# ScalarE's list of small jobs in the down product: the two relus of the big pass's lower right quarter moved ahead by two and one places, with an empty job between them

## The chip, the cores and the metric

One core of one Trainium2 chip. The time is device microseconds of one execution; the kernel before took a median of 957.89 us in 3 runs (957.74 to 960.14). The profile is of one further execution, whose span is 954.6 us.

## The reference, cut to what matters

```python
# x: (8, 4224, 192)
w = softmax(weight)                       # (8 heads, 7 taps)
x = sum over k of w[h, k] * x_padded[:, s + k, head h]     # causal convolution along s
mu, var = mean and variance of x over its 192 columns
xn = (x - mu) / sqrt(var + 1e-6) * g_ln
out = x + relu(xn @ w_ch1) @ w_ch2        # w_ch1: 192 x 768, w_ch2: 768 x 192
```

All in float32.

## The kernel before

The 8 x 4224 rows are cut into 18 groups: three small ones to start with and, from group 3 on, groups of 128 x 16 rows. For each group VectorE makes the convolution (L417, with ScalarE making the first two taps, L380 and L398), the rows are transposed in 32 x 32 blocks, TensorE makes the first product ("up", L533), the relu follows, TensorE makes the second product ("down", L850), and the result is scaled by 1/sqrt(var) (L929) and added to the output, where the convolution already stands, by a DMA that accumulates (L940).

For the groups from 3 on both products are made by a 2 x 2 block scheme in which seven products of quarters stand in for eight. In the up product (`up_mixed`) this is done in two passes: the small pass `one`, over one of three chunks of the hidden units, and after it the big pass `two`, over the other two. Each pass leaves four quarters of the hidden matrix in the tile `room`: c11, c12 (upper) and c21, c22 (lower). The quarter c22 of the big pass is put together from a copy out of PSUM (L651) and a second copy, which goes to a side tile called `parts_tb`, and which GpSimd's queue then adds into `room` by one accumulating DMA of 1024 KB (L609). A relu in place must follow that DMA. It is made by ScalarE (L664) in two halves of 128 x 1024, one for each of the big pass's two hidden chunks.

The down product (`down_fast`) is seven products, each of three output chunks (c = 0, 1, 2). A chunk of a product is 3 hidden chunks x 4 row blocks = 12 matmuls, which the profile records as 24, so that a product has 72 records. Inside an output chunk the hidden chunk of the small pass comes first, then the two of the big pass. The first product reads the upper left quarter, the second the lower left one, and the third the lower right one, c22, with all its relus made. After each output chunk ScalarE copies the PSUM bank away (L856), except after the fourth product. The second and third products use the same three banks: the third accumulates on what the second left, and so may write a bank only after ScalarE has copied it.

What else ScalarE has to do stands in a list of small jobs, `work`, from which `product` takes a written-out number of jobs right after the copy of each output chunk: `behind` = 3 jobs a chunk in the first product, 2 in the second, 2 in the third, 3 in the fourth, then 2 in the fifth and sixth until the list is empty. `up_mixed` makes the list's first part for groups 3 to 16 (14 groups; the last group, 17, has a list of its own): the relu of the small pass's c22, then the scalings of rows 2 to 15 of the group before (`scale_one`; after row 7 and the last row the rows go out by DMA), and the two halves of the big pass's c22 put in at a fixed place. `down_fast` appends 16 jobs for the first two taps of the group after next, 8 `first_tap` and 8 `second_tap`, where there is such a group. Engines run their instructions in the order in which the program issues them.

With the list before, the first product's nine places hold the small relu and scalings 2 to 9; the two halves are the two jobs after the copy of the second product's first chunk; scalings 10 to 15 and the taps follow.

Of the kernel before, what the change touches and what calls it, by code (L numbers as in the profile page):

```python
# [16 lines left out]
def kernel(  # L17
# [593 lines left out]
    def up_mixed(g, ahead, pending):  # L611
# [167 lines left out]
        work = [lambda: one.relu(one.c22)]  # L779
        work += [lambda j=j: scale_one(j) for j in range(2, done)]  # L780
        half = [lambda i=i: two.relu(two.c22[:, i : i + 1]) for i in range(PAIR)]
        return work[0:9] + half + work[9:]

    def down_row(rows, left):

# [210 lines left out]
    def ahead(g):  # L996


        if results is not None:
            for half in range(2):  # L1000
                finish_fast(g - 1, half, *results)
        yield
# [3 lines left out]
    for g in range(NG):  # L1006
# [3 lines left out]
        if mixed:  # L1010
            work = up_mixed(g, ahead(g), pending)
            pending = iter(())
        else:
            up(g)
            work = []
# [90 lines left out]
```

## Time and profile before

| what | value |
|---|---|
| time, median of 3 runs | 957.89 us (957.74 to 960.14) |
| span of the profiled execution | 954.6 us |
| TensorE busy (matmuls) | 946.8 us, 99% |
| VectorE busy | 894.2 us, 94% |
| ScalarE busy | 694.8 us, 73% |
| GpSimd busy | 341.8 us, 36% |
| relus L664, 128 x 1024 | 88 of 1063 ns |
| scalings L929, 128 x 192 | 224 of 464 ns |
| copies L856 to `cs`, 128 x 256 | 168 of 375 ns |
| taps L380 / L398, 128 x 384 | 120 of 634 ns / 112 of 638 ns |
| ScalarE's longest waits: L651 for TensorE (L533) | 98.6 us in 143 waits |

Busy time is the time in which an engine has an instruction running. The page's fourth part follows the work that ended last back to its releasers; its fifth lists groups of instructions with the mean time of one. A timeline gives, for one engine, the start and length of each group of like instructions in order, with the idle time just before it and what ended that. One instruction may start before the one ahead of it on its engine has ended, so a pair of 1.06 us can take 2.01 us.

### The profile page before, as it was taken

Reading aid. Unit: us, or ns where it says so; the run is one execution under the profiler, and the core shown is the slowest. Engines: PE = TensorE matmul, PEld = TensorE weight load, DVE = VectorE, ACT = ScalarE, POOL = GpSimd, SP = SyncE. Lnnn points to the kernel's source line nnn. Section 1 sums busy time; section 2 is a strip of 40 time slices with the busy share of each in tenths; the row PEclk is TensorE's granted clock in tenths of the full one; section 3 lists DMA queues with packets and bytes.
Section 4 is the critical chain, followed back from the end, with each engine's and each line's share of the span. In section 5 each row is a group of like instructions: output and inputs, shape, how many; then the busy total and the mean of one; then the engine's idle time right before and its main releaser. Section 6 shows DMA issues by size and latency. Waiting matters only on the chain.

```text
span 954.6 us, 37896 instructions
## 1 busy us (share of the span) xinstructions
PE 946.8 (99%) x16858; PEld 734.5 (77%) x16858; DVE 894.2 (94%) x1496; ACT 694.8 (73%) x1166; POOL 341.8 (36%) x474
## 2 busy tenths in 40 slices
PE   8999999999999999999999999999999999999998
PEld 7998896877869687786958778695867769586787
DVE  8999999999999999999999999999999999999867
ACT  7764678596877959687796968779695877967362
POOL 1158422613145141533227141452316232261330
PEclk9999999999999999999999999999999999999999
DMA  8359589689696988979697897969889697778261
GB/s 206 111 151 218 110 233 269 122 188 226 130 273 131 251 158 185 221 130 278 126 252 152 199 215 128 277 133 249 158 198 206 124 275 134 174 135 141 40 122 68
DMA packets 39832, 169.34 MB, mean 177 GB/s; under 512 B 4469, under 2 KB 8182, under 8 KB 33655
## 3 DMA queue, kind: packets, MB, share of 16 engines
q0 software_dynamic: 32864, 106.77, 60.2%
q1 hardware_dynamic: 6800, 60.16, 17.4%
q8 instruction: 132, 2.16, 0.9%
q14 instruction: 30, 0.25, 0.1%
q10 hardware_dynamic: 6, 0.00, 0.0%
HBM read 38.93 MB, written 50.33 MB: 94 GB/s over the span
## 4 chain that ended last, share of the span: by engine, by line
PE 96%; DMA 1%; POOL 1%; ACT 1%; issue 0%; DVE 0%; ACTq 0%; POOLq 0%
PE ps L533 46%; PE ps L850 44%; PE ps L787 4%; PE ps L367 1%; DMA room<-room 1%; DMA out_dram<-y 1%; PE ps L326 1%; ACT room L651 0%; POOL room L609 0%; POOL d L460 0%; ACT y L380 0%; POOL r L483 0%; POOL d L478 0%; POOL d L479 0%; PE ps L335 0%
## 5 line engine op out<-in xcount | busy, mean ns | idle before, releaser
L417 DVE SCALAR_TENSOR_TENSOR y<-xg,taps,y 128x384 f32<-128x384 f32 (+3 forms) x720 | 364.8, 583 | 2.6 <-DMA y<-room 1.4
L850 PE MATMUL ps<-room,w2sums 128*32 128x256 f32 (+2 forms) x4608 | 246.6, 371 | 0.0
L533 PE MATMUL ps<-yt,w 32*128 32x256 f32 (+2 forms) x4104 | 234.7, 378 | 1.0 <-ACT room L523 0.5
L533 PEld LDWEIGHTS ps<-yt,w 32*128 32x128 f32 x4104 | 204.2, 185 | 26.3 <-issue 8.7
L651 ACT COPY room<-ps 128x1024 f32<-128x1024 f32 (+1 forms) x129 | 169.0, 1310 | 74.5 <-PE ps L533 73.5
L850 PEld LDWEIGHTS ps<-room,w2sums 128*32 128x32 f32 x4608 | 149.3, 110 | 91.5 <-ACT room L664 5.3
L850 PE MATMUL ps<-room,w 128*32 128x256 f32 (+2 forms) x3456 | 188.9, 371 | 0.0
L817 DVE TENSOR_TENSOR room<-room 128x1024 f32<-128x1024 f32 (+2 forms) x147 | 161.2, 1170 | 22.6 <-PE ps L850 16.0
L850 PEld LDWEIGHTS ps<-room,w 128*32 128x32 f32 x3456 | 110.7, 110 | 70.3 <-DVE room L657 5.0
L533 PE MATMUL ps<-ysums,w1sums 32*128 32x256 f32 x2160 | 124.9, 379 | 0.2 <-issue 0.2
L533 PEld LDWEIGHTS ps<-ysums,w1sums 32*128 32x128 f32 x2160 | 109.5, 185 | 10.5 <-ACT room L651 3.3
L940 POOL DMA_DIRECT2D out_dram<-ot x69 | 59.0, 942 | 155.6 <-ACT ot L929 102.5
L409 POOL DMA_DIRECT2D y<-tb x59 | 52.5, 1386 | 153.5 <-ACT room L856 110.1
L856 ACT COPY cs<-ps 128x256 f32<-128x256 f32 (+2 forms) x192 | 70.1, 367 | 45.2 <-PE ps L850 45.2
L664 ACT ACTIVATE room<-room 128x1024 f32<-128x1024 f32 (+1 forms) x89 | 92.5, 1072 | 1.7 <-DMA room<-parts_cs 0.9
L929 ACT ACTIVATE ot<-ot,r 128x192 f32<-128x192 f32 x224 | 90.9, 464 | 0.0
L380 ACT ACTIVATE y<-xg,taps 128x384 f32<-128x384 f32 (+3 forms) x141 | 73.0, 607 | 1.0 <-DMA out_dram<-y 0.7
L448 DVE BATCH_NORM_STATS2 st<-y 128x6 f32<-128x192 f32 x264 | 70.1, 344 | 0.0
L856 ACT COPY room<-ps 128x256 f32<-128x256 f32 (+2 forms) x96 | 35.5, 370 | 45.8 <-PE ps L850 43.8
L398 ACT ACTIVATE tb<-xg,taps 128x384 f32<-128x384 f32 (+1 forms) x120 | 66.1, 628 | 0.0
L533 PE MATMUL ps<-yt,w1sums 32*128 32x256 f32 x1080 | 65.2, 380 | 0.6 <-ACT room L651 0.6
L533 PE MATMUL ps<-ysums,w 32*128 32x256 f32 x1080 | 64.5, 376 | 0.0
(119 smaller groups left out, 924.8 us busy)
## 6 DMA issues: line engine op xcount, KB each, us to landing
xg<-in_x_dram SPq DMA_DIRECT2D x14, 2112.0 KB, 16.4
room<-room POOLq DMA_DIRECT2D x45, 512.0 KB, 5.1
out_dram<-ot POOLq DMA_DIRECT2D x59, 384.0 KB, 9.6
y<-tb POOLq DMA_DIRECT2D x58, 384.0 KB, 8.4
out_dram<-y SPq DMA_DIRECT2D x13, 1536.0 KB, 8.8
room<-parts_cs POOLq DMA_DIRECT2D x28, 512.0 KB, 6.7
room<-parts_tb POOLq DMA_DIRECT2D x14, 1024.0 KB, 7.6
xg<-in_x_dram POOLq DMA_DIRECT2D x1, 2112.0 KB, 13.8
```

The lines of the kernel that those rows point to most:

```text
L380: nc.scalar.mul(y[g][:, 0:n, cs], xg[g][:, 0:n, cs], taps[:, h, 0:1])
L398: nc.scalar.mul(tb[g][:, 0:n, cs], xg[g][:, 1 : 1 + n, cs], taps[:, h, 1:2])
L417: nc.vector.scalar_tensor_tensor(out=y[g][:, 0:n, cs], in0=t[:, k : k + n, cs], scalar=taps[:, h, k : k + 1], in1=y[g][:, 0:n, cs], op0=AL ...
L448: nc.vector.bn_stats(out=sums[g][:, j, :], in_=y[g][:, j, :])
L533: nc.tensor.matmul(banks[:, q, i * w : i * w + w], right[rows, c, P * i : P * i + P], left[rows, :, c, :], start=(first and c == 0 and i = ...
L651: nc.scalar.activation(dst, src, AF.Relu) if relu else nc.scalar.copy(dst, src)
L664: nc.scalar.activation(c, c, AF.Relu)
L817: nc.vector.tensor_tensor(a[:, *dst, f], a[:, *left, f], a[:, *right, f], op=op)
L850: nc.tensor.matmul(dst[C * q : C * q + C, 0:w], right[:, f, C * c : C * c + C], left[:, f, q], start=(first and f == PAIR), stop=(f == PAI ...
L856: nc.scalar.copy(to[:, c], dst[:, 0:w].rearrange("p (j t) -> p j t", t=t))
L929: nc.scalar.mul(ots[g][:, j, :], ots[g][:, j, :], rstd[g][:, j : j + 1])
L940: nc.gpsimd.dma_start(out=rows[:, d0:d1], in_=src[:, d0:d1], accum_op=ALU.add)
```

## The change

Only the order in which `up_mixed` hands out its list is changed: 7 jobs instead of 9 stand before the first half, an empty job follows it, then the second half, then the rest.

```diff
         work = [lambda: one.relu(one.c22)]
         work += [lambda j=j: scale_one(j) for j in range(2, done)]
         half = [lambda i=i: two.relu(two.c22[:, i : i + 1]) for i in range(PAIR)]
-        return work[0:9] + half + work[9:]
+        return work[0:7] + [half[0], lambda: None, half[1]] + work[7:]
```

With `behind` = (3, 2, 2, 3) the first product's nine places now hold the small relu, scalings 2 to 7, the first half and the empty job; the second product's first chunk is followed by its copy, the second half and scaling 8; its second chunk by scalings 9 and 10; and so on. The list is longer by the empty job, so that each place further on holds the job that stood one place ahead of it.

## The prediction

> **What bounds the kernel now.** I read the page first: span, busy times, the chain that ended last.
>
> ```profile
> span 954.6 us, 37896 instructions
> PE 946.8 (99%) x16858; PEld 734.5 (77%) x16858; DVE 894.2 (94%) x1496; ACT 694.8 (73%) x1166; POOL 341.8 (36%) x474
> PEclk9999999999999999999999999999999999999999
> PE 96%; DMA 1%; POOL 1%; ACT 1%; issue 0%; DVE 0%; ACTq 0%; POOLq 0%
> ```
>
> TensorE sets the end: 96% of the chain is its matmuls, at a granted clock of 0.9 or more throughout. A change on ScalarE can only be worth the time in which TensorE stands or is held back. So I read the list of waits next, for weight loads (PEld) that wait for the moved relus (L664).
>
> ```profile
> PEld ps L850 <- ACT room L664: 5.3, 14, 0.4
> ```
>
> There are 14 such waits, one in each of the groups 3 to 16, 5.3 us together, 0.38 us each. The weight loader runs ahead of the matmuls, so its idle time isn't TensorE's loss. For that I took the timeline of TensorE in one down product, that of the pass from 533.55 us, and of its weight loads (columns: start, length, engine, line, work, count, idle before).
>
> ```profile
> 533.55 4.09 PE L850 MATMUL ps<-room,w 128*32 128x256 f32 x72
> 537.46 8.06 PE L850 MATMUL ps<-room,w2sums 128*32 128x256 f32 x144
> 545.34 4.07 PE L850 MATMUL ps<-room,w 128*32 128x256 f32 x72
> 549.22 7.95 PE L850 MATMUL ps<-room,w2sums 128*32 128x256 f32 x144
> 556.99 4.07 PE L850 MATMUL ps<-room,w 128*32 128x256 f32 x72
> ...
> 537.24 4.66 PEld L850 LDWEIGHTS ps<-room,w2sums 128*32 128x32 f32 x88
> 542.29 2.75 PEld L850 LDWEIGHTS ps<-room,w2sums 128*32 128x32 f32 x56 [0.38 <-ACT room L664]
> ```
>
> Take differences of starts. Products five and six (144 records) take 556.99 - 549.22 = 7.77 us, product four 549.22 - 545.34 = 3.88. Products two and three, the same count as five and six, take 545.34 - 537.46 = 7.88. So the wait costs TensorE 7.88 - 7.77 = 0.11 us a pass. It stands where 88 loads are made: 72 of product two and 16 of product three, that is 8 for the small pass's hidden chunk and 8 for the first half. What is late is the second half's relu, before the load at 542.29. ScalarE in the same pass:
>
> ```profile
> 538.67 0.36 ACT L856 COPY cs<-ps 128x256 f32<-128x256 f32 x1
> 538.93 1.15 ACT L929 ACTIVATE ot<-ot,r 128x192 f32<-128x192 f32 x3
> 539.98 0.36 ACT L856 COPY cs<-ps 128x256 f32<-128x256 f32 x1
> 540.23 2.01 ACT L664 ACTIVATE room<-room 128x1024 f32<-128x1024 f32 x2
> 542.14 0.36 ACT L856 COPY cs<-ps 128x256 f32<-128x256 f32 x1
> ...
> 530.67 0.86 POOL L609 DMA_DIRECT2D room<-parts_tb  x1 [6.86 <-ACT parts_tb L651]
> ...
> DMA to landing us min/median/max: 7.0/7.6/8.8
> ```
>
> The pair of halves ends at 540.23 + 2.01 = 542.24 us and the load starts at 542.29. Above it stand scalings 7, 8, 9 (three in 1.15 us). None of these lines has an idle time in front: ScalarE is behind its work here, not waiting. The last lines are the issue of the DMA that must land before the first half, and the landing times of the 14 such DMAs from their issue.
>
> **The change part by part.** Nothing is computed less or more: the same relus, scalings, copies and taps, in another order.
>
> *What is taken from in front of the second half.* Steps of ScalarE from start to start, by the same lines: a copy 0.25 us (539.98 to 540.23), a scaling 0.35 ((1.15 - 0.46)/2, a scaling being 464 ns), a half relu 0.95 (2.01 - 1.06). New order after the copy at 538.67: scaling 7 at 538.93, first half at 539.28, copy of product two's first chunk at 540.23, second half at 540.48, which ends at 541.54. Then scaling 8 at 541.43, the copy of the second chunk at 541.78, scalings 9 and 10, and the copy of the third at 542.73.
>
> *What TensorE needs.* Product three would start at 537.46 + 3.88 = 541.34. Its 17th matmul comes 16/72 of 3.88 later, at 542.20, and its load 0.22 ahead of that (537.24 against 537.46 at the start of product two), at 541.98. The second half ends at 541.54: 0.44 us early, so that wait is gone. Three others come near it. The first load of product three, at 541.12, needs the first half and the copy of the first chunk's bank, over by 540.23 + 0.36 = 540.59: 0.53 early. The second chunk's bank is needed 8 records of 0.054 us after 541.98, at 542.41; its copy ends at 542.14: 0.27 early. The third's is needed at 543.70 and is copied by 543.09. So the whole 0.11 us goes and nothing takes its place: 14 x 0.11 = 1.5 us.
>
> *The DMA in front of the first half.* This wait is not new, but it now comes sooner: 539.28 - 530.67 = 8.61 us after the issue instead of 9.56. Behind it on ScalarE queue up the three copies for whose banks TensorE waits. The landing took 7.6 us (median), so there is 1.0 us to spare. At the longest, 8.8, the half would wait 0.2 us, which the 0.27 of the tightest copy covers. Cost taken: nothing. If that cover were gone it is one for one: landings of 8.9 us and more hold TensorE.
>
> The Trainium skill ("DMA: Bandwidth & Descriptors", Rules for kernel authors) speaks against this part: issue a DMA early, do compute, wait on its semaphore late. The same page's fit, 2.0 us plus bytes over 436e3 per us, would make 1 MiB land in an estimated 4.4 us, and the sum by it is the same 1.5 us gained. The traced 7.6 decides, and with it the rule still has 1.0 us in hand.
>
> *What is delayed.* Scalings 8 and 9 and all behind them stand further down the list. The copies come 0.25 to 0.5 us sooner, since each place holds one job less before it; the scaling of row 11 and of row 15, after which GpSimd sends rows out, come some 0.25 us later. GpSimd waited in these places for ScalarE anyway (the DMA issues at 543.49 and 545.41), nothing else is queued on it before the taps' DMAs, and VectorE writes the next results (L914) late enough, in the pass from 422.75 us at 452.65 against the last issue at 434.61, 18 us for a landing of 9.6: cost nothing. The taps: as many jobs stand ahead of the first one as before (17) and ahead of the last one too (32), so they are made at the same time; where a copy of products three and five moves, it moves ahead of one tap, to be 0.5 us earlier. SP's queue is not touched.
>
> *What follows a freed TensorE.* VectorE's sums (L817) start when product three ends. VectorE idles 1.02 us there, having ended its transpose at 544.19 for a start at 545.21, so it starts 0.11 sooner and the later products, which wait for these sums, move along. The rest of the pass depends on TensorE alone, and the 1.5 us reach the end.
>
> The sum: 954.6 - 1.5 = 953.1 us of span. Around the span the runs have 957.89 - 954.6 = 3.3 us; so the median goes to 957.89 - 1.5 = 956.4. That is 0.16%, less than the 0.3% (2.9 us) that a measurement of this kernel can tell from no change.
>
> **The bounds.** Both unknowns come from this trace. The gain a pass is 0 if the next copy takes the wait's place, and 0.11 if none does. One pass in this execution had a late DMA on ScalarE (0.99 us before L651 at 748.74, and a TensorE period of 56.3 us against 55.4); whether it happens again changes the time by 0.9 either way. Range: 957.89 - 1.5 - 0.9 = 955.5 below, and no gain with half of that late DMA above, 957.89 + 0.45 = 958.3.
>
> **The rivals.**
>
> *The wait only changes its name: 957.9.* The copy of product two's second chunk has 0.27 us to spare by steps taken from other pairs of neighbours; a relu between two copies isn't in the trace as such. If a copy after a relu came 0.3 us later than reckoned, the load for the second chunk would wait instead. For it: ScalarE is behind throughout this stretch. Against it: in the old order the same copy ended at 542.50 and even that wasn't shown as a wait after the one at 542.29.
>
> *The whole idle time of the loader is gained: 957.9 - 5.3 = 952.6.* For it: the row of waits has 5.3 us, and a loader that is ahead might keep TensorE denser. Against it: TensorE's own starts lose only 0.11, not 0.38, and its matmuls are back to back at 3.88 a product elsewhere. The Trainium skill ("TensorE: Matmul & The Clock Gate", The mechanism) says that weight loads are pulled ahead of running matmuls in a window of 64; by that alone the 0.38 would be wholly hidden and the gain 0, while the trace shows a lead of 0.22 and a loss of 0.11.
>
> *Slower: the first half waits for its DMA, 966.6.* One mechanism, at the first half: from a landing of 8.88 us after issue (8.61 + 0.27) each further microsecond is one on TensorE, 14 times. If the DMA landed as the other accumulating ones of this queue do (`out_dram<-ot`, 9.6 us), it would be 14 x (9.6 - 8.88) = 10.1 us lost against 1.5 gained: 957.9 + 8.6. It decides the sign against 0.3% from a mean landing of 8.88 + (2.9 + 1.5)/14 = 9.2. For it: the queue carries much at that time. Against it: 14 landings between 7.0 and 8.8, and no DMA of the output is issued before the half that wasn't before.
>
> **How the numbers follow.** Forecast (1.5 us gained, 956.4) 0.74; the wait changes its name 0.13; both are within 0.3%, 0.87 together. The larger gain 0.07, which is all of faster. The late DMA 0.06, all of slower. The time is that of the forecast; the range 955.5 to 958.3 takes in the first two cases and leaves the others out.
>
> **What would show it.** In the changed kernel's profile the waits of weight loads at L850 for L664 should be gone from the list, with none for L856 in their place; products two and three should take 7.77 us by their starts; ScalarE should show copy, scaling, relu, copy, relu, scaling, copy without idle time; the period from pass to pass should be 55.29 us instead of 55.40. I am wrong if ScalarE idles before L664 for `parts_tb`, if a weight load waits for L856, or if the products shorten by 0.11 and the end doesn't move, which would mean that another engine holds the pass.

## The result, and the profile after

The changed kernel took 955.51 us (median of 11 runs, 954.57 to 956.52), the kernel before, beside it and earlier, 957.5 us (median of 11, 955.96 to 960.14). The ratio is 0.998, with a 95% interval of 0.9972 to 0.9988: 2.0 us less, by the interval 1.1 to 2.7. Two further comparisons of the same two kernels gave 0.9984 (0.9975 to 0.9992) and 0.9981 (0.9972 to 0.9991). The predicted gain was 1.5 us, 0.9984 of the median before; the forecast was 956.4 us and the range 955.5 to 958.3, so that the median lies just inside its lower end. The interval stays below 1, so 11 runs of each kernel do tell 0.2% from no change, for which the prediction had thought 0.3% necessary.

The page of the changed kernel: span, busy times, the chain that ended last.

```profile
span 953.1 us, 37882 instructions
PE 946.6 (99%) x16858; PEld 742.9 (78%) x16858; DVE 894.4 (94%) x1496; ACT 694.9 (73%) x1166; POOL 341.0 (36%) x474
PE 99%; DVE 0%; DMA 0%; issue 0%; ACT 0%
```

TensorE's matmuls are 99% of the chain, and ScalarE is as busy as it was. From the list of waits of the changed kernel, all the rows of weight loads of the down product (columns: who waited for whom, us in total, times, longest):

```profile
PEld ps L850 <- DVE room L657: 5.0, 15, 0.3
PEld ps L850 <- ACT y L380: 0.4, 1, 0.4
PEld ps L850 <- issue: 0.3, 1, 0.3
PEld ps L850 <- ACT room L651: 0.3, 1, 0.3
```

The row with L664 (5.3 us in 14 waits) is gone, and no row with L856 has come. TensorE and its weight loads in one pass, the timelines of the changed kernel from 533.74 us:

```profile
533.74 4.09 PE L850 MATMUL ps<-room,w 128*32 128x256 f32 x72
537.64 7.95 PE L850 MATMUL ps<-room,w2sums 128*32 128x256 f32 x144
545.41 4.07 PE L850 MATMUL ps<-room,w 128*32 128x256 f32 x72
549.30 7.95 PE L850 MATMUL ps<-room,w2sums 128*32 128x256 f32 x144
557.07 4.07 PE L850 MATMUL ps<-room,w 128*32 128x256 f32 x72
...
537.43 7.68 PEld L850 LDWEIGHTS ps<-room,w2sums 128*32 128x32 f32 x144
```

Products two and three take 545.41 - 537.64 = 7.77 us by their starts, as five and six do; before it was 7.88. The 144 weight loads are one group without an idle time in it. ScalarE in the same pass of the changed kernel:

```profile
538.85 0.38 ACT L856 COPY cs<-ps 128x256 f32<-128x256 f32 x1
539.10 0.47 ACT L929 ACTIVATE ot<-ot,r 128x192 f32<-128x192 f32 x1
539.46 1.06 ACT L664 ACTIVATE room<-room 128x1024 f32<-128x1024 f32 x1
540.41 0.38 ACT L856 COPY cs<-ps 128x256 f32<-128x256 f32 x1
540.66 1.08 ACT L664 ACTIVATE room<-room 128x1024 f32<-128x1024 f32 x1
541.62 0.46 ACT L929 ACTIVATE ot<-ot,r 128x192 f32<-128x192 f32 x1
541.97 0.38 ACT L856 COPY cs<-ps 128x256 f32<-128x256 f32 x1
```

This pass begins 533.74 - 533.55 = 0.19 us later than the one on which the steps were made. With that taken off, the first half starts at 539.27 (reckoned 539.28), the second at 540.47 (540.48), the copy of the second chunk at 541.78 (541.78).

### The profile page after: what moved, and what is told of

Same layout as the page of the kernel before. It is cut to its first block, busy times and chain, and to the rows that moved or that the text cites. A ratio compares the mean times of both kernels' runs of the same rounds, so it can differ in the third digit from the quotient of the medians.

```text
span 953.1 us, 37882 instructions
## 1 busy us (share of the span) xinstructions
PE 946.6 (99%) x16858; PEld 742.9 (78%) x16858; DVE 894.4 (94%) x1496; ACT 694.9 (73%) x1166; POOL 341.0 (36%) x474
## 4 chain that ended last, share of the span: by engine, by line
PE 99%; DVE 0%; DMA 0%; issue 0%; ACT 0%
PE ps L533 49%; PE ps L850 44%; PE ps L787 4%; PE ps L367 1%; PE ps L326 1%; PE ps L354 0%; DVE yt L428 0%; PE ps L335 0%; PE ps L357 0%; PE ps L340 0%; DMA room<-in_weight_dram 0%; PE ps L960 0%; PE ps L211 0%; DVE y L944 0%; ACT y L330 0%
## 5 line engine op out<-in xcount | busy, mean ns | idle before, releaser
L850 PE MATMUL ps<-room,w2sums 128*32 128x256 f32 (+2 forms) x4608 | 245.0, 371 | 0.0
L850 PEld LDWEIGHTS ps<-room,w2sums 128*32 128x32 f32 x4608 | 153.4, 110 | 85.7
L850 PE MATMUL ps<-room,w 128*32 128x256 f32 (+2 forms) x3456 | 188.9, 371 | 0.0
L850 PEld LDWEIGHTS ps<-room,w 128*32 128x32 f32 x3456 | 112.7, 110 | 68.2 <-DVE room L657 5.0
L856 ACT COPY cs<-ps 128x256 f32<-128x256 f32 (+2 forms) x192 | 70.3, 368 | 45.1 <-PE ps L850 45.0
L664 ACT ACTIVATE room<-room 128x1024 f32<-128x1024 f32 (+1 forms) x89 | 94.4, 1072 | 2.5 <-DMA room<-parts_cs 1.1
L929 ACT ACTIVATE ot<-ot,r 128x192 f32<-128x192 f32 x224 | 94.6, 467 | 0.0
L856 ACT COPY room<-ps 128x256 f32<-128x256 f32 (+2 forms) x96 | 35.2, 369 | 44.0 <-PE ps L850 43.3
```

The lines of the kernel that those rows point to most:

```text
L664: nc.scalar.activation(c, c, AF.Relu)
L850: nc.tensor.matmul(dst[C * q : C * q + C, 0:w], right[:, f, C * c : C * c + C], left[:, f, q], start=(first and f == PAIR), stop=(f == PAI ...
L856: nc.scalar.copy(to[:, c], dst[:, 0:w].rearrange("p (j t) -> p j t", t=t))
L929: nc.scalar.mul(ots[g][:, j, :], ots[g][:, j, :], rstd[g][:, j : j + 1])
```

## The experiments

Each edit stands against the changed kernel's last line of `up_mixed`. All compute the same work, in another order. Theory A is the prediction's: TensorE loses what a relu or a bank copy comes after the matmul that needs it, the weight loader's lead being cover, and nothing else in the change counts.

### Both halves one place later, no empty job (e1_one_place)

```diff
-        return work[0:7] + [half[0], lambda: None, half[1]] + work[7:]
+        return work[0:8] + half + work[8:]
```

> The halves stand one place later than in the changed kernel and one sooner than before: scalings 7 and 8 and the first half after the first product's last copy, the second half after the copy of the second product's first chunk, no empty job. Theory A (TensorE loses only what the second half, or a bank copy, comes after the matmul that needs it, the weight loader's lead of 0.22 us being cover): in the steps of the pass from 533.55 us the second half ends at 541.89 against a load due at 541.98, and the copy of the second chunk at 542.49 against a load due at 542.41 and a matmul due at 542.63. So a short wait of the loader for L856, about 0.1 us, and nothing lost: products two and three 7.77 us, time as the changed kernel's within 0.5 us, 1.5 us below before. Theory B (any wait of the loader is paid): 0.1 x 14 = 1.4 us above the changed kernel.

954.74 us against 957.13, ratio 0.9978 (0.9969 to 0.9987). TensorE and its weight loads in the pass from 532.86 us, in the timelines of this kernel:

```profile
536.77 7.95 PE L850 MATMUL ps<-room,w2sums 128*32 128x256 f32 x144
544.54 1.69 PE L850 MATMUL ps<-room,w 128*32 128x256 f32 x28
...
536.56 5.09 PEld L850 LDWEIGHTS ps<-room,w2sums 128*32 128x32 f32 x96
541.87 2.37 PEld L850 LDWEIGHTS ps<-room,w2sums 128*32 128x32 f32 x48 [0.22 <-ACT cs L856]
```

The wait has come back under another name, L856, where it was reckoned to: after 96 loads, at the bank of the second chunk. It is 0.22 us in place of 0.1. Yet products two and three take 544.54 - 536.77 = 7.77 us here, and in all 14 passes: a wait no longer than the loader's lead costs nothing. Theory B, by which any wait of the loader is paid, falls.

### Without the empty job (e2_no_empty)

```diff
+        return work[0:7] + half + work[7:]
```

> The changed kernel without the empty job, so that both halves come ahead of the copy of the second product's first chunk. Theory A: that copy then starts at 541.18 and ends at 541.54, while product three wants to write its bank at 541.34; with 0.05 us of signalling TensorE loses 0.25 to 0.27 us a pass, products two and three take 8.04 us, a wait of weight loads for L856 takes the place of that for L664, and the time is 14 x 0.27 = 3.8 us above the changed kernel, 2.2 us above before. Rival (the empty job does not matter, only how early the relus are): as the changed kernel, 1.5 us below before.

959.54 us against 957.13, ratio 1.0025 (1.0016 to 1.0035): 2.4 us above before, where 2.2 were expected. TensorE and its loads in the pass from 534.40 us of this kernel:

```profile
538.31 8.23 PE L850 MATMUL ps<-room,w2sums 128*32 128x256 f32 x144
546.36 0.83 PE L850 MATMUL ps<-room,w 128*32 128x256 f32 x12
...
542.44 3.61 PEld L850 LDWEIGHTS ps<-room,w2sums 128*32 128x32 f32 x72 [0.55 <-ACT cs L856]
```

546.36 - 538.31 = 8.05 us (expected 8.04). The second half is earlier here than in the changed kernel (it ends 3.82 us after the start of product two, there 4.09), and the kernel is slower than before, because the copy of the first chunk's bank now stands behind both. The empty job is what lets that copy in between.

### Only an empty job (e3_only_empty)

```diff
+        return work[0:9] + half + [lambda: None] + work[9:]
```

> The order before with only an empty job put in after the two halves: relus where they were, all later jobs one place later, the copies behind them 0.35 us sooner. Theory A: the second half is as late as before, products two and three take 7.88 us and the time is that of before within 0.5 us. Rival C (the gain comes from the copies, which have one job less before them, and not from the relus): 1.5 to 2 us below before.

956.49 us against 957.13, ratio 0.9997 (0.9988 to 1.0005). The wait list and TensorE's timeline (pass from 533.56 us) of this kernel:

```profile
PEld ps L850 <- ACT room L664: 5.3, 14, 0.4
...
537.47 8.07 PE L850 MATMUL ps<-room,w2sums 128*32 128x256 f32 x144
545.35 4.07 PE L850 MATMUL ps<-room,w 128*32 128x256 f32 x72
```

545.35 - 537.47 = 7.88 us, as before. Making the copies from the third chunk's on sooner gains nothing by itself. The copy of the second chunk stands ahead of the empty job and isn't sooner here: it ends 5.05 us after the start of product two, 5.04 before.

### Only the relus moved (e4_only_relus)

```diff
+        def two_of(jobs):
+            for job in jobs:
+                job()
+
+        head = [half[0], lambda: None, half[1], work[7], lambda: two_of(work[8:10])]
+        return work[0:7] + head + work[10:]
```

> The relus stand as in the changed kernel, but two scalings share a place after the copy of the second product's second chunk, so that every later job stands where it stood before. Theory A: the whole gain, products two and three 7.77 us, 1.5 us below before. Rival C (the gain is the copies'): products two and three nearer to 7.88 us, at most half of the gain.

955.65 us against 957.13, ratio 0.9987 (0.9977 to 0.9996). TensorE in the pass from 532.73 us of this kernel (the edit adds five lines, so that L850 reads L855):

```profile
536.64 7.95 PE L855 MATMUL ps<-room,w2sums 128*32 128x256 f32 x144
544.41 4.07 PE L855 MATMUL ps<-room,w 128*32 128x256 f32 x72
```

7.77 us, so the gain in the products is all there with every later job where it stood. One copy moves along with the relus in e4 as in the changed kernel, that of the second chunk, which ends 4.69 us after the start of product two instead of 5.04. Whether the gain is its doing is settled by e1: there it ends at 5.04, as before, the second half alone is sooner (4.44 instead of 4.78), and products two and three take 7.77 us. With e1 and e3 this shows that the gain is the relus', and rival C falls. The median of 1.5 us less is what was expected.

### The first half four jobs earlier still (e5_half_early)

```diff
+        return work[0:3] + [half[0], work[3], lambda: None] + work[4:7] + [half[1]] + work[7:]
```

> The first half stands three jobs earlier still, right after the copy of the first product's second chunk, 6.95 us after the issue of its DMA; all else as in the changed kernel. Theory A with the DMA's price: the DMA lands 7.0 to 8.8 us after its issue, so ScalarE stands for 0.2 to 1.9 us before the first half in every pass, and what goes beyond the 0.42 us of cover (copy of the second product's second chunk) is TensorE's loss. With the 14 landings of the kernel before this makes 4.3 us: 3 to 6 us above the changed kernel, 1.5 to 4.5 above before, with the waits of weight loads for L856 or L664. Rival (ScalarE makes the time good, or TensorE has more cover): as the changed kernel within 1 us.

By the edit the half moves ahead of four scalings (rows 4 to 7), not three jobs; the 6.95 us are reckoned for that place. 961.22 us (5 runs) against 956.76, ratio 1.0047 (1.0034 to 1.0059): 4.5 us above before and 5.9 above the changed kernel on the same chip. From ScalarE's waits, ScalarE's timeline and TensorE's timeline of this kernel, the pass from 368.93 us:

```profile
ACT room L664 <- DMA room<-parts_tb: 7.9, 12, 1.7
...
372.74 0.37 ACT L856 COPY cs<-ps 128x256 f32<-128x256 f32 x1
374.32 1.06 ACT L664 ACTIVATE room<-room 128x1024 f32<-128x1024 f32 x1 [1.21 <-DMA room<-parts_tb]
...
372.83 4.07 PE L850 MATMUL ps<-room,w2sums 128*32 128x256 f32 x72
377.33 4.36 PE L850 MATMUL ps<-room,w2sums 128*32 128x256 f32 x72 [0.43 <-ACT cs L856]
381.51 0.83 PE L850 MATMUL ps<-room,w 128*32 128x256 f32 x12
```

ScalarE stands 1.21 us for the DMA, and products two and three take 381.51 - 372.83 = 8.68 us: 0.91 of the 1.21 is lost. Over the 14 passes they lose 3.9 us against 7.77 each, where 4.3 were reckoned from the landings of the kernel before; the six passes whose DMA landed soon lose nothing. In the other eight the loss is ScalarE's wait less 0.30 to 0.32 us, so the cover is a little less than the 0.42 reckoned. (One of the twelve waits in the row, of 1.04 us, is in the last group, where every kernel here has one of 0.5 to 1.0.) This profile also has 2.1 us in one pass in which TensorE waited for nothing that the profile shows (before a matmul at 666.06). The products' 3.9 us are thus shown; where the other 2 of the 5.9 come from, and whether the four runs without a profile have them in the same place, is not.

### The second half later (e6_half_late)

```diff
+        return work[0:9] + [half[0], lambda: None, half[1]] + work[9:]
```

> The order before, but an empty job between the two halves, so that the second half is made after the copy of the second product's second chunk: 0.25 us later than before. Theory A (a relu that is late is paid one for one once it is later than its matmul): it ends at 542.49, signalled at 542.54, against a matmul due at 542.20: 0.36 us lost a pass, products two and three 8.13 us, 14 x 0.25 = 3.5 us above before, 5.0 above the changed kernel. Rival (the wait before was paid only in part, 0.11 of 0.38, and so is a longer one): 0.63 x 0.3 = 0.19 a pass, 1.1 us above before.

961.41 us (5 runs) against 956.76, ratio 1.0047 (1.0034 to 1.0061): 4.7 us above before by the medians, 3.3 to 5.8 by the interval, where 3.5 were expected. TensorE in the pass from 534.57 us of this kernel:

```profile
538.48 4.93 PE L850 MATMUL ps<-room,w2sums 128*32 128x256 f32 x88
543.58 3.23 PE L850 MATMUL ps<-room,w2sums 128*32 128x256 f32 x56 [0.17 <-ACT room L664]
546.63 3.64 PE L850 MATMUL ps<-room,w 128*32 128x256 f32 x64
```

546.63 - 538.48 = 8.15 us (expected 8.13). The second half came 0.27 us later than before (it ends 5.05 us after the start of product two instead of 4.78), and products two and three grew by 0.27, or 3.8 us in 14 passes: once the lead is used up, a late relu is paid one for one. A wait that is paid by a fixed share of it would have given 1.1 us, which the interval excludes.

### The changed kernel again, and beside the order one place later (e7_after_again, e8_one_place_again, e9_after_beside)

> The changed kernel once more, beside the others. Theory A: 1.5 us below before, 953 us of span where no late DMA holds ScalarE. Rival (part of the measured 2.0 us came from the runs of before having more late DMAs than usual): nearer to 1.5 than to 2.0 if it was chance, 2.0 again if the change removes something besides the wait.

955.32 us against 956.76, ratio 0.9984 (0.9975 to 0.9992): 1.5 us, so nothing speaks for a gain besides the wait's.

> The order with the halves one place later than in the changed kernel, again, now beside the changed kernel on one chip. Theory A: products two and three take 7.77 us in both, so the two are equal within 0.5 us; what the first comparison had between them, 0.6 to 0.8 us in favour of this order, is chance or another chip. Rival D: the first half, 0.35 us further from its DMA, stands ScalarE less, and this order is 0.5 us or more faster again.

> The changed kernel beside the order with the halves one place later. Theory A: equal to it within 0.5 us, 1.5 us below before. In both profiles the first down product of the large groups began at another time (146.6 and 146.8 us in two of the changed kernel, 145.2 in the other order), ahead of all that was changed: if that is the program's, it comes again; if it is chance, the starts will lie within the 144.9 to 146.8 us that the runs so far show, in either order.

On one chip the order one place later took 954.97 us, ratio 0.9987 (0.9978 to 0.9996), the changed kernel 955.1 us, ratio 0.9981 (0.9972 to 0.9991), against 956.42 before. The medians differ by 0.1 us, so rival D is not borne out, though 11 runs of each cannot exclude half a microsecond; no order tried here beats the changed kernel by more than the runs can tell. The first down product of the large groups began at 145.5 us in the order one place later and at 146.3 in the changed kernel. The changed kernel's three starts are the three latest of eleven profiles, but the part in which the time goes differs: in the first two it is before TensorE's work at L335 (12.7 and 12.6 us against 10.1 to 10.8 elsewhere), in the third L335 comes at 10.1 and the time goes after it. What sets this opening, which lies ahead of everything the change moves, was not looked into. In the order one place later, two passes of one profile and three of the other take 0.2 to 0.3 us more than the 55.29 us of the others; beside the changed kernel on one chip that, 0.67 us in all, about makes up for the opening, which is 0.78 us shorter. The three profiles of the changed kernel have no such pass. In e4 one pass takes 0.7 us more. Whether that belongs to the order or to chance stays open.

## Why the prediction was right

*What is gained and where.* The step "14 x 0.11 = 1.5 us" holds pass by pass: 7.88 to 7.77 us in each of the 14. It goes on as reckoned: VectorE's sums start 545.29 - 533.74 = 11.55 us into the pass instead of 545.21 - 533.55 = 11.66, and the period from pass to pass is 55.29 us (one of 55.36) instead of 55.40. A clean sum of it comes from the stretch that the change can touch, from the first to the last down product of the large groups. In e3, where the wait is as before, it is 921.01 - 145.74 = 775.27 us; in the changed kernel's three profiles it is 773.7 us each time (in the first 920.37 - 146.64 = 773.73). The difference is 1.54 us.

*The span was hit for more than its reason.* 953.1 us was predicted and measured, but the two profiles differ by more than the wait. Before, that stretch was 921.86 - 145.59 = 776.27 us, a full microsecond over e3's, most of which is the one late DMA that the prediction had put in its bounds. It didn't come in the changed kernel, whose opening was in turn 1.05 us longer. The two chances nearly cancelled. For the runs, gains of 1.9, 1.5 and 1.8 us by the ratios of three comparisons are one and the same within their intervals. That 955.51 still lay in the range, by 0.01 us, was luck: of the 0.9 us below the forecast 0.4 come from the kernel before itself, which took 957.89 us in 3 runs and 957.5 in 11; the other 0.5 are within the noise.

*What TensorE needs.* All three due times held. In the changed kernel the copy with the least to spare, the second chunk's, makes no wait in any pass of the first profile; moved 0.35 us later in e1, it makes one of 0.22, and moved past the matmul's own due time, as the first chunk's copy is in e2, it is paid for. So the rival in which the wait only changes its name was a matter of a few tenths: it is what e1 shows, harmlessly, and what e2 shows at a price.

*The DMA ahead of the first half.* Its cost was taken as nothing, with cover of 0.27 us beyond 8.61 us after issue. The changed kernel's 14 landings were 7.0 to 8.8 us (median 7.6), as before. One of its two late ones shows the cover at work: in the pass from 367.80 us, ScalarE's and TensorE's timelines and the landing.

```profile
373.17 0.48 ACT L929 ACTIVATE ot<-ot,r 128x192 f32<-128x192 f32 x1
373.77 1.06 ACT L664 ACTIVATE room<-room 128x1024 f32<-128x1024 f32 x1
...
371.71 7.95 PE L850 MATMUL ps<-room,w2sums 128*32 128x256 f32 x144
379.48 1.90 PE L850 MATMUL ps<-room,w 128*32 128x256 f32 x30
...
DMA to landing us min/median/max: 8.8/8.8/8.8
```

The first half starts 0.60 us after the scaling instead of 0.36, so ScalarE stood 0.24 us, and products two and three still take 379.48 - 371.71 = 7.77. In the changed kernel's second profile (e7) the same pass had a landing of 8.9 us. There ScalarE idled 0.21 us before the half and one weight load waited 0.19 us for L856, both named in the prediction as signs of being wrong; yet products two and three took 7.77 us. The 0.27 us were reckoned up to the load, and the loader's lead comes on top, so "landings of 8.9 us and more hold TensorE" put the limit too early. The rule to wait late for a DMA, weighed in the prediction, is right in kind here: e5, which waits 1.7 us sooner than the changed kernel, pays for it in the passes with a late landing. The slower rival was thus a true mechanism whose point of decision the change stops short of.

*The larger gain* (all of the loader's 5.3 us) is excluded by the products: 0.11 a pass, no more. That weight loads pulled ahead would hide the wait wholly is excluded as well. Waits of the loader of 0.38 us (before), 0.55 (e2) and 0.66 (e6) cost TensorE 0.11, 0.28 and 0.38, so 0.27 to 0.28 us of each was hidden, and the 0.22 of e1 wholly. That is 0.05 us more than the lead of 0.22 by which the prediction counted; why is not shown. The section of the Trainium skill that the prediction cites for the pull-ahead ("TensorE: Matmul & The Clock Gate", The mechanism) ties it to loads into a row group that doesn't conflict or into the background weight buffer, which the prediction leaves out; no run here shows which of these held.

*What was said to cost nothing.* The rows went out 0.27 us later (the third DMA of rows 10.22 us after the pass's start in place of 9.94), the taps' DMAs were issued at 21.03 us in both, and e3 and e4 show no price or gain of the shifted jobs that these runs can tell from none.

## What to carry to other kernels

A wait in the list of an engine that runs ahead is worth only what is left of it after the lead: compare the starts of the engine behind over a stretch with an undisturbed stretch of the same work, and count that, 0.11 us here and not 0.38. To move a late job forward, write out the start-to-start steps of its engine and the due time of each job it passes; one job too far (e2) turned a gain of 1.5 us into a loss of 2.4. When a predicted time is hit, check the sum over the stretch that was changed, since unrelated parts of a profile move by a microsecond.

## What was not expected of the hardware

The opening of the kernel, the same in all of these programs, took between 144.9 and 146.8 us in eleven profiles, more than the change is worth, while the stretch from the first to the last large group repeated to 0.01 us in the changed kernel's three profiles (773.73, 773.74, 773.73) and was 774.3 and 774.4 in those of the order one place later.
